# Last stage of an attention, PReLU and soft-mixture kernel: VectorE block transposes, nine output buffers, and unread identity products between the last products

## The chip, the core and the metric

The kernel runs as one program on one core of a Trainium2 chip. The metric is the device time of one execution in microseconds (us), lower is better; three runs of the kernel before are known. A profile of one further execution shows every engine: TensorE (PE, with its weight loads apart as PEld), VectorE (DVE), ScalarE (ACT), GpSimd (POOL) and SyncE (SP), which issues all DMAs.

## What is computed

Three layers in fp32, for 4608 tokens of 512 features:

```python
q_p, k_p = phi(q), phi(k)                # exp features, 8 batches x 8 heads x 576 tokens
x = (q_p @ (k_p.T @ v)) / (q_p @ z)      # linear attention
h = x @ w_in
g = np.maximum(h, 0.0) + alpha * np.minimum(h, 0.0)
x = g @ w_out
logits = x @ phi                         # 32 slots: 8 experts x 4
d = softmax(logits, axis=0)              # over the tokens
slot_input = d.T @ x                     # 32 x 512
h = np.maximum(slot_input[e] @ w1[e], 0.0)
slot_out[e] = h @ w2[e]                  # per expert, 4 slots each, w1 512x1024, w2 1024x512
c = softmax(logits, axis=1)              # over the slots
out = c @ slot_out                       # 4608 x 512
```

## The kernel before

The tokens are taken in 12 blocks of 384. In a slot, one of 16 columns of `w_in` is multiplied with a block (L505), put through the leaky function on ScalarE and VectorE into `gT`, and block-transposed on VectorE into `gb` (L532); the dispatch softmax keeps running sums in `acc` and `lsum`, which each block rescales by `sc` (products `pS`, L602, added at L614). This loop takes nearly the whole time. The text here is on what follows the last block.

- **The reduction.** After the last block's logits (`pl` L540, `pr` L558) VectorE transposes `dT` into `d`, TensorE forms `pS` (96 products of 32x32 tiles), VectorE adds them into `acc` (L614), and TensorE sums the four quarters of `acc` with a folding matrix `tident` (`pg`, L757), each followed by a ScalarE copy to `aT` (L759). `px` (L762) multiplies with `w_out`; `lsum` scales it (L768); `psi` (L769) folds it into the slot inputs `sT`.
- **The experts.** `pe` (L782) multiplies `sT` with `w1`: 64 products of 128 rows by 512 columns into four column strips of the array. ScalarE applies the ReLU (L784), TensorE turns the result (`pth`, L790), and VectorE places each expert's own four slots into a zeroed `hTm` (L793). `pso` (L819) multiplies with `w2`, 64 products of 256 columns for each half `dh` of the output features.
- **The output.** The combine weights (`combine`, on VectorE) are split into high and low halves (`cr`, L803, L805), turned on TensorE (`pc`, L808) and copied to `cT` (L810). For each half, `so` (L823) and `prp` (L825) give `sor`, and 36 products `po` (L836) of one weight load and 256 columns each go out over copies into `os` (L839 and L841, 512 columns each) and one 512 KB DMA for each of nine `os` tiles (L842). `os` has three buffers.

All DMAs stand in one queue, SP's, in the program's order. `fetch` (L686) loads the weights in 144 pieces of 256 KB: 16 of `w_out`, 64 of `w1`, 64 of `w2`. The first 100 go to buffers that the loop has left; the last 44, all of `w2`, wait for buffers of earlier pieces that have been read, in the order that `reuse` gives. The output's DMAs stand behind them.

`spin(count, before)` (L105) issues products of the identity with itself that nobody reads, chained to their neighbours by `together`, so that TensorE is not idle. The order of instructions on each engine is made by the scheduler of the framework from its own model of times.

Of the kernel before, what the change touches and what calls it, by code (L numbers as in the profile page):

```python
# [9 lines left out]
F32 = mybir.dt.float32  # L10
# [16 lines left out]
BT = 384  # L27
# [16 lines left out]
SPIN = [5, 3, 13, 6]  # L44

F64_LEAST = struct.unpack("<f", struct.pack("<I", 0x38100000))[0]
# [15 lines left out]
def attention_prelu_softmoe(ctx: ExitStack, tc, qT, kT, v, wphi, w_in, w_out, alpha, phi, w1, w2, out):  # L62
# [39 lines left out]
    def spin(count, before):  # L102
        turn = bank("spin", ps_d)
# [33 lines left out]
    acc = const.tile([128, 4, 512], F32, name="acc")  # L137
# [409 lines left out]
    gemm_last, spun = [None], [None]  # L547

    def softmax(step, n):
# [39 lines left out]
        def turn():  # L589
            d = st["d"] = sm.tile([128, 512], F32, tag="d", name="d")[:, 0:BT]  # L590
            nc.vector.transpose(out=d, in_=st["dT"])
            for r in range(4):
                sl = slice(32 * r, 32 * r + 32)
                nc.vector.transpose(  # L594
                    out=logits[sl, TB * n:TB * n + TB, :],
                    in_=st["pr"][sl, 0:BT].rearrange("p (t r i) -> p t r i", t=TB, r=4)[:, :, r])

        def gather():
            two = banks("pS")
            pS = st["pS"] = [bank("pS"), bank("pS"), two[:, 0], two[:, 1]]  # L600
            last = together([
                lambda j=j, i=i, h=h: nc.tensor.matmul(  # L602
                    pS[i][32 * (j % 4):32 * (j % 4) + 32, 256 * h:256 * h + 256], st["d"][32 * i:32 * i + 32, 32 * j:32 * j + 32],
                    gb[n, h][32 * i:32 * i + 32, :, 32 * j:32 * j + 32], start=(j < 4), stop=(j >= 4 * TB - 4))
                for h in (1, 0) for j in range(4 * TB) for i in range(4)], spun[0] if n == NB - 1 else None)
            if n == NB - 1:
                spun[0] = spin(SPIN[3], last)

        def add():
            for i in range(4):  # L610
                if st["first"]:
                    nc.vector.tensor_copy(acc[:, i], st["pS"][i])
                else:
                    nc.vector.scalar_tensor_tensor(out=acc[:, i], in0=acc[:, i], scalar=st["sc"], in1=st["pS"][i], op0=ALU.mult, op1=ALU.add)  # L614
# [5 lines left out]
        at_step(step + 2, "pe2", gather)  # L620
        at_step(step + 2, "post", add)
# [37 lines left out]
    at(NC * (NB - 1) - 6, "post", lambda: combine(0, NT - 2 * TB))  # L659
    at(NC * (NB - 1) + 8, "post", lambda: combine(NT - 2 * TB, NT - TB))  # L660
# [5 lines left out]
    pieces += [("w2", dh, e, c) for dh in range(2) for e in range(E) for c in range(EF // 256)]  # L666
    got, groups = {}, []

    def fetch(pool, tag, count=1, bufs=1, whole=None):
# [3 lines left out]
        for i in range(count):  # L673
# [8 lines left out]
            else:  # L682
                _, dh, e, c = key
                t = t.rearrange("p (c d) -> p c d", c=2)
                src = w2[e, 256 * c:256 * c + 256, 256 * dh:256 * dh + 256].rearrange("(c p) d -> p c d", p=128)
# [56 lines left out]
    kept = ["klo", "kraw", "khi", "vte", "vto", "kp1", "ks", "pf0", "pf1", "kp2", "pf2", "pf10", "pf11", "pf12", "pf13", "w8", "w9", "w10", "gb", "gT"]  # L742
# [8 lines left out]
    pg, px, psi = bank("pg"), bank("px"), bank("psi")  # L751
    sT = sm.tile([128, BT], F32, tag="dT", name="sT")[:, 0:KD * NSL].rearrange("p (k s) -> p k s", k=KD)
    aT = sm.tile([128, 512], F32, tag="d", name="aT")
    for i in range(4):
        o = slice(128 * i, 128 * i + 128)
        spun[0] = together([
            lambda c=c: nc.tensor.matmul(pg[:, 128 * i + 32 * c:128 * i + 32 * c + 32], acc[:, i, 128 * c:128 * c + 128], tident[:, 0:32], start=True, stop=True)  # L757
            for c in range(4)], spun[0])
        nc.scalar.copy(aT[:, o], pg[:, o])  # L759
    for i in range(4):  # L760
        spun[0] = together([
            lambda c=c: nc.tensor.matmul(  # L762
                px[32 * c:32 * c + 32, :], aT[:, 128 * i + 32 * c:128 * i + 32 * c + 32], got["wo", 4 * i + c], start=(i == 0), stop=(i == 3))
            for c in range(4)], spun[0])
    acc = acc[:, 0]
    for k in range(KD):
        o = slice(128 * k, 128 * k + 128)
        nc.scalar.activation(acc[:, o], px[:, o], AF.Identity, scale=lsum)  # L768
        nc.tensor.matmul(psi[:, 32 * k:32 * k + 32], acc[:, o], tident[:, 0:32], start=True, stop=True)  # L769
        nc.scalar.copy(sT[:, k, :], psi[:, 32 * k:32 * k + 32])  # L770

    hTm = [attk.tile([128, 4, E, NSL], F32, tag="kp2", name="hTm", bufs=KPB) for f in range(2)]
    for t in hTm:
        nc.gpsimd.memset(t, 0.0)
    hrs = attk.tile([128, 2, 512], F32, tag="kp2", name="hrs", bufs=KPB)
    hr_t = {}
    for eg in range(2):
        for fh in range(2):
# [4 lines left out]
            hr = hr_t[eg, fh] = hrs[:, fh, :]  # L783
            nc.scalar.activation(hr, pe, AF.Relu)  # L784
            if (eg, fh) == (0, 0):
                continue
            for g2, f2 in ([(0, 0), (0, 1)] if (eg, fh) == (0, 1) else [(eg, fh)]):
                pt = bank("pth")
                for c in range(4):
                    nc.tensor.transpose(pt[:, 128 * c:128 * c + 128], hr_t[g2, f2][:, 128 * c:128 * c + 128], ident)  # L790
                for j in range(4):
                    e = 4 * g2 + j
                    nc.vector.tensor_copy(  # L793
                        hTm[f2][:, :, e, 4 * e:4 * e + 4],
                        pt.rearrange("p (c s) -> p c s", c=4)[:, :, 32 * j + 4 * e:32 * j + 4 * e + 4])

    combine(NT - TB, NT)
    cT_t = []
    for i in range(NT // 4):
        cr = pf.tile([128, 4, 4, NSL], F32R, tag=f"pf{PF - 4 + i % 2}", name="cr")  # L800
        lg = logits[:, 4 * i:4 * i + 4, :]
        for r in range(2):
            nc.vector.tensor_copy(cr[:, :, r, :], lg)  # L803
        for r in range(2):
            nc.vector.tensor_tensor(out=cr[:, :, 2 + r, :], in0=lg, in1=cr[:, :, r, :], op=ALU.subtract)  # L805
        pc = bank("pc").rearrange("p (t s) -> p t s", t=4)
        for t in range(4):
            nc.tensor.transpose(pc[:, t, :], cr[:, t].rearrange("p r s -> p (r s)").bitcast(F32), ident)  # L808
        cT = (attk if i < 7 else pf).tile([128, 4, 128], F32R, tag=kept[i], name="cT")
        nc.scalar.copy(cT, pc)  # L810
        cT_t.append(cT)

    so2 = pf.tile([128, 2, 256], F32, tag="pf12", name="so")
    sor2 = pf.tile([128, 2, 256], F32R, tag="pf13", name="sor")
    for dh in range(2):
        pso = (ps_l, ps_d)[dh].tile([128, 512], F32, tag="ld"[dh], name="pso")[:, 0:256]
        for e in range(E):
            for c in range(EF // 128):
                nc.tensor.matmul(  # L819
                    pso[32 * (c % 4):32 * (c % 4) + 32, :], hTm[c // 4][:, c % 4, e, :], got["w2", dh, e, c // 2][:, c % 2, :],  # L820
                    start=(e == 0 and c < 4), stop=(e == E - 1 and c >= 4))
# [6 lines left out]
        for r in (1, 3):  # L828
            sl = slice(32 * r, 32 * r + 32)
            nc.vector.tensor_tensor(out=sor[sl], in0=prp[sl], in1=sor[sl], op=ALU.subtract)  # L830
        for i in range(NT // 4):
            os_ = wring.tile([128, 4, 256], F32, tag=f"w{8 + i % 3}", name="os")
            for t2 in range(2):
                po = (ps_h.tile([128, 512], F32, tag="h", name="po") if (2 * i + t2) % 2 else bank("po"))
                for t in range(2):
                    nc.tensor.matmul(po[:, 256 * t:256 * t + 256], cT_t[i][:, 2 * t2 + t, :], sor, start=True, stop=True)  # L836
                pv = po.rearrange("p (t d) -> p t d", t=2)
                if t2:
                    nc.vector.tensor_copy(os_[:, 2:4], pv)  # L839
                else:  # L840
                    nc.scalar.copy(os_[:, 0:2], pv)  # L841
# [56 lines left out]
```

## Time and profile before

| | |
|---|---|
| three runs | 1056.34, 1056.88, 1061.24 us (median 1056.88) |
| profiled execution | 1057.16 us, its span 1055.4 us |
| busy share of the span | PE 93%, DVE 73%, ACT 45%, POOL 14% |
| mean granted TensorE clock | 0.964 of 2.4 GHz |
| DMA | 110.60 MB |

The span is from the first to the last instruction of the program; times below are counted from its start. A busy PE is not a PE at its peak, as products are pipelined and their ends are modelled; the distance between two starts is the better measure.

### The profile page before, as it was taken

The page shows a single profiled execution, that of the slowest core. Times are in us where ns is not written, and L with a number is a line of the kernel's source. Part 1 is how long each engine was busy: PE and PEld are TensorE (multiplying, and loading weights), DVE is VectorE, ACT ScalarE, POOL GpSimd, SP SyncE. Part 2 cuts the span into 40 slices and gives each one's busy share as a digit, 9 for nine tenths or more (in the row PEclk, how much of TensorE's full clock was granted, in tenths as well). Part 3 has the DMA queues.
Part 4 walks back from the last instruction along what each step waited for, and adds up shares of the span by engine and source line. Part 5 has one row for each costly group of instructions (what it writes and reads, how often), then busy time and mean ns, then how long its engine had stood idle before and what let it go on. Part 6 is the DMA issues. An engine that isn't in the chain of part 4 may idle for free.

```text
span 1055.4 us, 21864 instructions
## 1 busy us (share of the span) xinstructions
PE 984.1 (93%) x9038; PEld 685.2 (65%) x9038; DVE 773.8 (73%) x1552; ACT 469.8 (45%) x908; POOL 149.2 (14%) x88
## 2 busy tenths in 40 slices
PE   3787998998999999999999999999999999998994
PEld 1445776774676776676666776767667767787353
DVE  3999989879767578587878687687888486874133
ACT  3876867776444245144235344343334343200133
POOL 2201214121111212121112111121112221000000
PEclk7898999998999999999999999999999999999995
DMA  5343653653010111010401111110401200769879
GB/s 199 120 141 125 193 188 114 225 178 100 9 31 31 39 31 38 20 51 19 163 10 38 32 39 31 31 38 19 160 19 46 96 8 2 249 226 327 261 235 309
DMA packets 71986, 110.60 MB, mean 105 GB/s; under 512 B 7248, under 2 KB 47312, under 8 KB 71888
## 3 DMA queue, kind: packets, MB, share of 16 engines
q1 hardware_dynamic: 71888, 109.22, 32.0%
q8 instruction: 71, 1.16, 0.4%
q14 instruction: 27, 0.22, 0.1%
HBM read 89.27 MB, written 19.92 MB: 103 GB/s over the span
## 4 chain that ended last, share of the span: by engine, by line
PE 71%; DVE 3%; DMA 2%; ACT 1%; issue 1%; DVEq 0%; ACTq 0%; SPq 0%
PE ph L505 34%; PE num L435 5%; PE pS L602 5%; PE pkv L333 5%; PE pl L540 4%; PE den L442 3%; PE pq L403 3%; PE pk L289 2%; DMA out_dram<-os 2%; PE pso L819 1%; PE pe L782 1%; PE sel L477 1%; PE pt L355 1%; PE pr L558 1%; PE densum L460 1%; PE pkv L339 1%
## 5 line engine op out<-in xcount | busy, mean ns | idle before, releaser
L505 PE MATMUL ph<-xhi,w 128*128 128x384 f32 x1536 | 435.2, 351 | 6.5 <-DVE gT L515 4.4
L505 PEld LDWEIGHTS ph<-xhi,w 128*128 128x128 f32 x1536 | 279.0, 189 | 76.8 <-issue 41.5
L505 PE MATMUL ph<-xlo,w 128*128 128x384 f32 x768 | 255.1, 340 | 0.0
L415 POOL PARTITION_ALL_REDUCE mb<-pj x48 | 140.4, 2928 | 553.0 <-ACT pj L409 450.1
L505 PEld LDWEIGHTS ph<-xlo,w 128*128 128x128 f32 x768 | 143.6, 188 | 12.6 <-issue 6.1
L515 DVE SCALAR_TENSOR_TENSOR gT<-gT,alpha_neg,ph 128x384 f32<-128x384 f32 x104 | 62.9, 605 | 77.3 <-ACT ph L514 76.5
L532 DVE STREAM_TRANSPOSE gb<-gT 128x384 f32<-128x384 f32 x192 | 105.6, 566 | 5.7 <-DMA gT<-gT_d 1.9
L513 ACT ACTIVATE gT<-ph 128x384 f32<-128x384 f32 x104 | 50.8, 489 | 114.8 <-PE ph L505 114.0
L425 ACT ACTIVATE qe<-pj 128x768 f32<-128x768 f32 x92 | 73.9, 839 | 59.5 <-DVE pj L419 56.2
L517 DVE TENSOR_SCALAR gT<-ph,alpha_sb 128x384 f32<-128x384 f32 x88 | 53.8, 613 | 46.2 <-PE ph L505 45.8
L333 PE MATMUL pkv<-kp,vt 128*64 128x256 f32 (+1 forms) x640 | 85.0, 400 | 1.1 <-DVE wpr L250 1.1
L435 PE MATMUL num<-qe,kv 128*64 128x192 f32 (+1 forms) x496 | 70.9, 417 | 0.0
L283 ACT ACTIVATE kp<-kp 128x512 f32<-128x512 f32 (+1 forms) x80 | 46.8, 586 | 51.6 <-DVE kp L282 51.1
L333 PEld LDWEIGHTS pkv<-kp,vt 128*64 128x64 f32 (+1 forms) x640 | 41.3, 140 | 39.4 <-issue 17.1
L280 DVE TENSOR_REDUCE mx<-pk 128x4 f32<-128x512 f32 (+1 forms) x80 | 50.2, 627 | 11.4 <-PE pk L289 9.7
L602 PE MATMUL pS<-gb,d 32*32 32x256 f32 x2304 | 55.0, 385 | 0.3 <-DVE logits L594 0.2
L403 PE MATMUL pq<-qraw,wp 64*128 64x384 f32 x192 | 48.9, 562 | 6.7 <-DMA qraw<-in_qT_dram 4.1
L446 ACT COPY num<-num 128x384 f32<-128x384 f32 x48 | 22.8, 475 | 67.1 <-PE num L435 64.2
L409 ACT COPY pj<-pq 128x768 f32<-128x768 f32 x44 | 35.2, 799 | 36.3 <-PE pq L403 36.3
L419 DVE TENSOR_TENSOR pj<-pj,mb 128x768 f32<-128x768 f32 x48 | 46.6, 971 | 6.0 <-POOL mb L415 6.0
L282 DVE TENSOR_TENSOR kp<-pk,mx 128x512 f32<-128x512 f32 (+1 forms) x80 | 50.2, 627 | 0.8 <-PE pkv L333 0.2
L514 ACT ACTIVATE ph<-ph 128x384 f32<-128x384 f32 x104 | 50.6, 487 | 0.0
(191 smaller groups left out, 1345.6 us busy)
## 6 DMA issues: line engine op xcount, KB each, us to landing
w<-in_w_dram SPq DMA_DIRECT2D x58, 256.0 KB, 5.7
qraw<-in_qT_dram SPq DMA_DIRECT2D x48, 192.0 KB, 2.4
out_dram<-os SPq DMA_DIRECT2D x18, 512.0 KB, 3.7
raw<-in_w_in_dram SPq DMA_DIRECT2D x16, 512.0 KB, 3.6
raw<-in_w_out_dram SPq DMA_DIRECT2D x16, 512.0 KB, 4.2
gT_d<-gT SPq DMA_DIRECT2D x32, 192.0 KB, 2.0
gT<-gT_d SPq DMA_DIRECT2D x8, 768.0 KB, 5.2
pf<-in_w_dram SPq DMA_DIRECT2D x21, 256.0 KB, 6.0
```

Of the source, the lines that this page charges most:

```text
L333: return lambda: nc.tensor.matmul(pkv[64 * j:64 * j + 64, 0:256], vt[:, 64 * j:64 * j + 64], feats(t, j).rearrange("p s f -> p (s f)"), st ...
L403: lambda j=j, sl=slice(64 * j, 64 * j + 64): nc.tensor.matmul(pq[j][:, 0:BT], wp[sl], st["qraw"][sl], start=True, stop=True)
L415: nc.gpsimd.partition_all_reduce(mb, pj, 128, bass_isa.ReduceOp.absmax)
L425: nc.scalar.activation(st["e", s], pj, AF.Exp, scale=(1.0, -1.0)[s])
L435: lambda s=s, j=j: nc.tensor.matmul(num[64 * j:64 * j + 64, o:o + w], kvs[:, s, 64 * j:64 * j + 64], st["e", s][:, j, o:o + w], start=(s = ...
L505: gemm_last[0] = nc.tensor.matmul(h, (w_in_hi, w_in_lo)[a][c][:, 128 * k:128 * k + 128], (xhi, xlo)[b][:, k, :], start=(i == 0), stop=(i = ...
L513: nc.scalar.activation(gT, h, AF.Relu, scale=-1.0)
L514: nc.scalar.activation(h, h, AF.Relu)
L515: nc.vector.scalar_tensor_tensor(out=gT, in0=gT, scalar=alpha_neg[:, c:c + 1], in1=h, op0=ALU.mult, op1=ALU.add)
L517: nc.vector.tensor_scalar(out=gT, in0=h, scalar1=0.0, scalar2=alpha_sb[:, c:c + 1], op0=ALU.min, op1=ALU.mult)
L532: nc.vector.transpose(out=gb[n, c // 8][:, c % 8, :], in_=gT)
L602: lambda j=j, i=i, h=h: nc.tensor.matmul(pS[i][32 * (j % 4):32 * (j % 4) + 32, 256 * h:256 * h + 256], st["d"][32 * i:32 * i + 32, 32 * j: ...
```

## The change

It rebuilds what follows the last block, in these parts:

1. The old `acc` is rescaled on TensorE before the last `pS` (`carry`: products `pa` of `acc` with `tsc`, which is `tident` times `sc`), and `pS` is copied into `acc` on both engines and folded into the same `pa`. `pg` is four transposes, copied in two halves.
2. The ReLU and the masking of foreign slots are one VectorE instruction (`own` holds the mask, ten small reductions); the turns of `pth` and `pc` on TensorE become 32x32 block transposes on VectorE, and `combine` leaves its result block-transposed in `logits`. `pso` takes the rows of `w2` in another order, so each piece is read from DRAM with other strides: a partition's two rows of 1 KB, the next partition 64 KB on.
3. `po` multiplies without the split in halves: `sor` and `logits` are plain fp32, each product has 32 rows, and two stand side by side in different row strips of the array, into two banks. Behind each pair stand three identity products into a bank that nobody reads (`SPIN[8]`). Two copies of 256 columns follow each pair, one on each engine.
4. `os` has nine buffers, `w7` to `w15`; the pieces of `w2` that wait go into other ones, and the buffers of `w_out` come first.
5. More identity products stand in the reduction (`SPIN[3]` to `SPIN[7]`).

```diff
-SPIN = [5, 3, 13, 6]
+SPIN = [5, 3, 8, 3, 8, 5, 5, 5, 3]
...
+        def carry():
+            tsc = sm.tile([128, BT], F32, tag="ls", name="tsc")[:, 0:32]
+            nc.vector.tensor_scalar(out=tsc, in0=tident[:, 0:32], scalar1=st["sc"], scalar2=None, op0=ALU.mult)
+            pa = last["pa"] = ps_h.tile([128, 512], F32, tag="h", name="pa")
+            spun[0] = spin(SPIN[3], together([
+                lambda i=i: nc.tensor.matmul(pa[32 * i:32 * i + 32, :], tsc, acc[i], start=True, stop=False)
+                for i in (3, 2, 1, 0)], spun[0]))
+            gather()
+            for i in range(4):
+                (nc.scalar.copy if i % 2 else nc.vector.tensor_copy)(acc[i], st["pS"][i])
...
-        nc.vector.tensor_tensor(out=lg, in0=lg, in1=wide, op=ALU.mult)
...
+        for t in range(first, last, 16):
+            ts = slice(t, min(t + 16, last))
+            w = sm.tile([128, 512], F32, tag="gT", name="cw", bufs=5).rearrange("p (t s) -> p t s", s=NSL)[:, 0:ts.stop - t]
+            nc.vector.tensor_tensor(
+                out=w, in0=logits[:, ts], in1=cm[:, ts].unsqueeze(2).to_broadcast([128, ts.stop - t, NSL]), op=ALU.mult)
+            nc.vector.transpose(out=logits[:, ts], in_=w)
...
-                src = w2[e, 256 * c:256 * c + 256, 256 * dh:256 * dh + 256].rearrange("(c p) d -> p c d", p=128)
...
+                src = w2[4 * eg:4 * eg + 4].rearrange("e (f b) d -> (e f) b d", b=32)[:, 2 * b:2 * b + 2, 256 * dh:256 * dh + 256]
...
-    kept = ["klo", "kraw", "khi", "vte", "vto", "kp1", "ks", "pf0", "pf1", "kp2", "pf2", "pf10", "pf11", "pf12", "pf13", "w8", "w9", "w10", "gb", "gT"]
+    kept = ["kp2", "pf12", "pf13", "gb", "gT"] + [f"w{c}" for c in range(7, NC)]
...
+    pa = last["pa"]
+    spun[0] = spin(SPIN[5], together([
+        lambda i=i: nc.tensor.matmul(pa[32 * i:32 * i + 32, :], tident[:, 0:32], acc[i], start=False, stop=True)
+        for i in range(4)], spun[0]))
...
+    spun[0] = spin(SPIN[6], together([
+        lambda c=c: nc.tensor.transpose(pg[:, 128 * c:128 * c + 128], acc[c // 2][:, 128 * c:128 * c + 128], ident)
+        for c in range(4)], spun[0]))
+    nc.scalar.copy(aT[:, half[0]], pg[:, half[0]])
+    nc.vector.tensor_copy(aT[:, half[1]], pg[:, half[1]])
+    spun[0] = spin(SPIN[7], together([
+        lambda i=i, c=c: nc.tensor.matmul(
+            px[32 * c:32 * c + 32, :], aT[:, 128 * c + 32 * i:128 * c + 32 * i + 32], got["wo", 4 * i + c], start=(i == 0), stop=(i == 3))
+        for i in range(4) for c in range(4)], spun[0]))
...
-            nc.scalar.activation(hr, pe, AF.Relu)
...
+                out=hr[:, 512 * fh:512 * fh + 512], in0=pe, scalar1=0.0, scalar2=own[:, 4 + eg:5 + eg], op0=ALU.max, op1=ALU.min)
...
+                out=t[b].rearrange("p (b s) -> p b s", s=32),
+                in_=hr.rearrange("p (f b) -> p b f", b=32)[:, 16 * b:16 * b + 16])
...
-            nc.tensor.transpose(pc[:, t, :], cr[:, t].rearrange("p r s -> p (r s)").bitcast(F32), ident)
...
-    sor2 = pf.tile([128, 2, 256], F32R, tag="pf13", name="sor")
+    sor2 = pf.tile([128, 2, 256], F32, tag=f"pf{PF - 1}", name="sor")
...
-            os_ = wring.tile([128, 4, 256], F32, tag=f"w{8 + i % 3}", name="os")
-            for t2 in range(2):
-                po = (ps_h.tile([128, 512], F32, tag="h", name="po") if (2 * i + t2) % 2 else bank("po"))
-                for t in range(2):
-                    nc.tensor.matmul(po[:, 256 * t:256 * t + 256], cT_t[i][:, 2 * t2 + t, :], sor, start=True, stop=True)
...
+            os_ = wring.tile([128, 4, 256], F32, tag=f"w{7 + i}", name="os")
+            for h in range(2):
+                k = (2 * i + h) % 3
+                two = banks("po") if k == 2 else None
+                po = [two[:, j] if k == 2 else bank("po") if k else ps_h.tile([128, 512], F32, tag="h", name="po") for j in range(2)]
+                last[dh] = spin(SPIN[8], together([
+                    lambda j=j, r=2 * h + j, sl=slice(64 * h + 32 * j, 64 * h + 32 * j + 32): nc.tensor.matmul(
+                        po[j][:, 0:256], logits[sl, 4 * i:4 * i + 4, :].rearrange("p t s -> p (t s)"), sor[sl], start=True, stop=True)
+                    for j in range(2)], last.get(dh)), idle)
+                for j in range(2):
+                    (nc.vector.tensor_copy if j else nc.scalar.copy)(os_[:, 2 * h + j], po[j][:, 0:256])
```

Names of tiles in the rows that follow are the program's own; a number behind one is a buffer's.

On TensorE, the kernel before ends its second half of `pso` and then issues the two output halves in one piece each:

```order
L819 MATMUL pso<-w_10248,hTm 32x256 x4
L819 MATMUL pso<-w_10251,hTm 32x256 x4
L819 MATMUL pso<-w_10254,hTm 32x256 x4
L836 MATMUL po<-sor,cT 128x256 x36
L825 MATMUL prp<-so,tident 128x256
L836 MATMUL po<-sor,cT 128x256 x36
```

At the same place the changed kernel has:

```order
L828 MATMUL pso<-num,acc_112 32x256 x6
L828 MATMUL pso<-rhl,acc_113 32x256 x2
L828 MATMUL pso<-densel,acc_113 32x256 x2
L828 MATMUL pso<-w_10248,acc_113 32x256 x3
L846 MATMUL po<-sor,logits 128x256 x2
L106 MATMUL idle<-ident 128x128 x3
L846 MATMUL po<-sor,logits 128x256 x2
L106 MATMUL idle<-ident 128x128 x3
```

The last two rows come 18 times in all, and only then follow the last 25 products of the second half's `pso`, its `prp`, and 18 such pairs again. So the first output half now stands ahead of the end of `pso` on TensorE.

On TensorE after the last block's logits, the kernel before has:

```order
L558 MATMUL pr<-ls,tident 128x384
L105 MATMUL spin<-ident 128x128 x13
L602 MATMUL pS<-gb,d 32x256 x96
L105 MATMUL spin<-ident 128x128 x6
L757 MATMUL pg<-tident,acc 128x32 x16
```

and the changed kernel:

```order
L559 MATMUL pr<-ls,tident 128x384
L106 MATMUL spin<-ident 128x128 x8
L623 MATMUL pa<-acc_114,tsc 32x512
L623 MATMUL pa<-acc_113,tsc 32x512
L623 MATMUL pa<-acc_112,tsc 32x512
L623 MATMUL pa<-acc_111,tsc 32x512
L106 MATMUL spin<-ident 128x128 x3
L604 MATMUL pS<-gb,d 32x256 x96
L106 MATMUL spin<-ident 128x128 x8
```

`pS` now stands behind four products that read `tsc`, and behind three identity products.

On VectorE at that place the changed kernel has the rows below; before, `mrun`, `d`, `logits` and `lsum` followed `sc` with nothing between them.

```order
L579 TENSOR_TENSOR sc<-mrun,nm 128x1
L800 TENSOR_REDUCE own<-ident 128x1 x3
L580 TENSOR_TENSOR mrun<-mbl,mrun 128x1
L800 TENSOR_REDUCE own<-ident 128x1
L802 TENSOR_REDUCE own<-own 128x1
L592 STREAM_TRANSPOSE d<-dT 128x384
L596 STREAM_TRANSPOSE logits<-pr 32x128 x2
L588 SCALAR_TENSOR_TENSOR lsum<-lsum,sc,rs 128x1
L596 STREAM_TRANSPOSE logits<-pr 32x128
L620 TENSOR_SCALAR tsc<-tident,sc 128x32
```

Five reductions moved ahead of `d`, and `tsc` stands last.

## Rows read from the trace of the kernel before

**Rows 1.** By stage: us, busy us of PE, PEld, DVE, ACT, POOL, PEclk, DMA share, GB/s

```profile
966.00:981.30 15.30, 12.29 (x76) 7.95 (x76) 2.67 (x4) 1.06 (x4) 0.00 (x0) 0.78 0.76 242
...
1000.10:1022.80 22.70, 22.70 (x304) 12.36 (x303) 7.46 (x39) 6.25 (x11) 0.00 (x0) 1.00 0.80 253
1022.80:1055.40 32.60, 16.99 (x74) 13.32 (x74) 13.63 (x21) 10.73 (x19) 0.00 (x0) 0.66 0.87 290
```

**Rows 2.** Chain of waits after the loop: start us, us, what (x instructions)

```profile
961.97 3.99 PE pS L602 x173
...
968.08 1.83 issue
...
976.30 5.02 PE px L762 x32
...
984.88 0.34 PE psi L769 x2
...
987.41 3.57 PE pe L782 x32
...
1000.72 1.86 PE pso L819 x32
...
1017.44 0.59 PE pc L808 x4
...
1019.88 0.63 PE prp L825 x2
...
1022.79 1.63 PE po L836 x10
```

**Rows 3.** Waits after 950 us: who waited for whom: us, times, longest

```profile
ACT os L841 <- DMA out_dram<-os: 12.5, 11, 2.4
```

**Rows 4.** By stage again, a stretch of 4 us within the output

```profile
1044.00:1048.00 4.00, 2.97 (x10) 2.38 (x11) 1.80 (x3) 1.46 (x3) 0.00 (x0) 0.50 1.02 343
```

**Rows 5.** Timeline of TensorE at 956 us: start us, us, engine line op

```profile
956.60 0.94 PE L105 MATMUL spin<-ident 128*128 128x128 f32 x6
957.38 0.91 PE L558 MATMUL pr<-ls,tident 128*128 128x384 f32 x2
958.13 3.06 PE L105 MATMUL spin<-ident 128*128 128x128 f32 x26
961.12 0.40 PE L602 MATMUL pS<-gb,d 32*32 32x256 f32 x1
```

**Rows 6.** Timeline of TensorE at 399 us, a pair in row strips

```profile
399.18 0.34 PE L478 MATMUL sel<-rhl,densel 128*128 128x384 f32 x1
399.45 0.92 PE L403 MATMUL pq<-qraw,wp 64*128 64x384 f32 x4
400.30 0.44 PE L505 MATMUL ph<-xhi,w 128*128 128x384 f32 x1
```

**Rows 7.** Timeline of VectorE after 959 us

```profile
959.17 0.16 DVE L578 TENSOR_TENSOR sc<-mrun,nm 128x1 f32<-128x1 f32 x1
...
959.94 0.58 DVE L591 STREAM_TRANSPOSE d<-dT 128x384 f32<-128x384 f32 x1 [0.41 <-ACT dT L581]
...
962.81 0.25 DVE L654 TENSOR_REDUCE cm<-logits 128x3 f32<-128x96 f32 x1 [0.35 <-ACT logits L653]
```

**Rows 8.** Timeline of SP, the DMA issues

```profile
980.37 2.93 SPq L686 DMA_DIRECT2D vg<-in_w_dram  x6
...
993.03 19.86 SPq L686 DMA_DIRECT2D w<-in_w_dram  x26
```

**Rows 9.** DMA issues after 890 us: KB each, median us to landing

```profile
w<-in_w_dram SPq DMA_DIRECT2D x58, 256.0 KB, 5.7
out_dram<-os SPq DMA_DIRECT2D x18, 512.0 KB, 3.7
```

**Rows 10.** Timeline, copies of 256 columns

```profile
1012.26 0.42 DVE L823 COPY so<-pso 128x256 f32<-128x256 f32 x1 [0.65 <-PE pso L819]
...
1020.54 0.37 ACT L827 CAST sor<-prp 128x256 fp32r<-128x256 f32 x1 [1.89 <-PE prp L825]
```

More of the change, by code (lines that the diff above doesn't have):

```diff
@@ L100, in together, with spin @@
         return before
-    def spin(count, before):
-        turn = bank("spin", ps_d)
+    def spin(count, before, turn=None):
+        turn = turn or bank("spin", ps_d)
         return together([
@@ L136, in attention_prelu_softmoe @@
     wpr = sm.tile([128, NC, NSL], F32, tag="wpr", name="wpr")
-    acc = const.tile([128, 4, 512], F32, name="acc")
+    acc = [const.tile([128, 512], F32, name=f"acc{i}") for i in range(4)]
     lsum = const.tile([128, 1], F32, name="lsum")
@@ L546, in attention_prelu_softmoe @@
     first = [True]
-    gemm_last, spun = [None], [None]
+    gemm_last, spun, last = [None], [None], {}
     def softmax(step, n):
@@ L591, in turn @@
             nc.vector.transpose(out=d, in_=st["dT"])
-            for r in range(4):
-                sl = slice(32 * r, 32 * r + 32)
+            for i in range(TB):
+                g, j = divmod(TB * n + i, 4)
+                sl = slice(32 * j, 32 * j + 32)
                 nc.vector.transpose(
-                    out=logits[sl, TB * n:TB * n + TB, :],
-                    in_=st["pr"][sl, 0:BT].rearrange("p (t r i) -> p t r i", t=TB, r=4)[:, :, r])
+                    out=logits[sl, 4 * g:4 * g + 4, :],
+                    in_=st["pr"][sl, 128 * i:128 * i + 128].rearrange("p (t i) -> p t i", i=32))
         def gather():
@@ L600, in gather @@
             pS = st["pS"] = [bank("pS"), bank("pS"), two[:, 0], two[:, 1]]
-            last = together([
+            end = together([
                 lambda j=j, i=i, h=h: nc.tensor.matmul(
@@ L606, in gather @@
             if n == NB - 1:
-                spun[0] = spin(SPIN[3], last)
+                spun[0] = spin(SPIN[4], end)
         def add():
@@ L665, in attention_prelu_softmoe @@
     pieces += [("w1", eg, fh, k, j) for eg in range(2) for fh in range(2) for k in range(KD) for j in range(4)]
-    pieces += [("w2", dh, e, c) for dh in range(2) for e in range(E) for c in range(EF // 256)]
+    pieces += [("w2", dh, eg, i) for dh in range(2) for eg in range(2) for i in range(16)]
     got, groups = {}, []
@@ L760, in attention_prelu_softmoe @@
[L760 to L765, printed above, removed]
-    for k in range(KD):
[L767 to L776, printed above, removed]
-    for eg in range(2):
+    pa = last["pa"]
+    spun[0] = spin(SPIN[5], together([
+        lambda i=i: nc.tensor.matmul(pa[32 * i:32 * i + 32, :], tident[:, 0:32], acc[i], start=False, stop=True)
+        for i in range(4)], spun[0]))
+    half = [slice(0, 256), slice(256, 512)]
@@ new lines, in attention_prelu_softmoe @@
+    nc.scalar.copy(acc[0][:, half[0]], pa[:, half[0]])
+    nc.vector.tensor_copy(acc[1][:, half[1]], pa[:, half[1]])
+    pg, px, psi = bank("pg"), bank("px"), bank("psi")
+    spun[0] = spin(SPIN[6], together([
[7 more added lines that the diff above has]
+        for i in range(4) for c in range(4)], spun[0]))
@@ new lines, in attention_prelu_softmoe @@
+    nc.scalar.activation(acc[2][:, half[0]], px[:, half[0]], AF.Identity, scale=lsum)
+    nc.vector.tensor_scalar(out=acc[3][:, half[1]], in0=px[:, half[1]], scalar1=lsum, scalar2=None, op0=ALU.mult)
+    for k in range(KD):
+        nc.tensor.matmul(psi[:, 32 * k:32 * k + 32], acc[2 + k // 2][:, 128 * k:128 * k + 128], tident[:, 0:32], start=True, stop=True)
+    nc.scalar.copy(sT, psi[:, 0:KD * NSL].rearrange("p (k s) -> p k s", k=KD))
+    own = sm.tile([128, 8], F32, tag="sc", name="own", bufs=2)
@@ new lines, in attention_prelu_softmoe @@
+    for eg in range(2):
+        for j in range(4):
+            nc.vector.tensor_reduce(
+                out=own[:, j:j + 1], in_=ident[:, 36 * j + 16 * eg:36 * j + 16 * eg + 4], axis=AX.X, op=ALU.add)
+        nc.vector.tensor_reduce(out=own[:, 4 + eg:5 + eg], in_=own[:, 0:4], axis=AX.X, op=ALU.add)
+    nc.vector.tensor_scalar(out=own[:, 4:6], in0=own[:, 4:6], scalar1=F32_MOST, scalar2=None, op0=ALU.mult)
+    hT = []
+    for eg in range(2):
+        hr = attk.tile([128, EF], F32, tag="kp2", name="hr", bufs=KPB)
@@ L815, in attention_prelu_softmoe @@
+        hT.append(t)
+    combine(NT - 4, NT)
+    so2 = pf.tile([128, 2, 256], F32, tag=f"pf{PF - 2}", name="so")
+    sor2 = pf.tile([128, 2, 256], F32, tag=f"pf{PF - 1}", name="sor")
     for dh in range(2):
         pso = (ps_l, ps_d)[dh].tile([128, 512], F32, tag="ld"[dh], name="pso")[:, 0:256]
-        for e in range(E):
-            for c in range(EF // 128):
+        for eg in range(2):
+            for b in range(32):
                 nc.tensor.matmul(
-                    pso[32 * (c % 4):32 * (c % 4) + 32, :], hTm[c // 4][:, c % 4, e, :], got["w2", dh, e, c // 2][:, c % 2, :],
-                    start=(e == 0 and c < 4), stop=(e == E - 1 and c >= 4))
+                    pso[32 * (b % 4):32 * (b % 4) + 32, :], hT[eg][b // 16][:, 32 * (b % 16):32 * (b % 16) + 32],
+                    got["w2", dh, eg, b // 2][:, b % 2, :], start=(eg == 0 and b < 4), stop=(eg == 1 and b >= 28))
```

66 lines of the change are left out of this document (17 added, 49 removed).

## The prediction

> **What bounds the kernel now.** Only what follows the last block changes much, so I read the stages of the tail first, then its chain of waits, then the rows from which the new instructions can be priced. Between 1000.1 and 1022.8 us TensorE is busy without a gap, at the full clock, while the DMAs have room [rows 1]: there TensorE's own list of instructions is the bound. From 1022.8 us to the end it is the other way round: TensorE is busy for half of the time, and the copies wait for the output's DMAs, ScalarE's alone 12.5 us in eleven waits, because `os` has three buffers [rows 1, 3]. The DMAs then move 343 GB/s [rows 4], which is 1.53 us for one `os` of 512 KB, 27.5 us for eighteen. The reader is to see that the present output stage of 32.6 us is 27.5 us of DMA and 5 us of starting, turning from one half to the other, and landing. A change that adds TensorE work there costs nothing until an `os` takes TensorE more than 1.53 us.
>
> **The price of a pass.** A fp32 product runs as two passes. 26 identity passes of 128 columns take 2.99 us up to the next product's start [rows 5], and the last of them includes a change to another tiling of the array. A change costs 0.10: from `sel` to `pq` it is 0.27 us [rows 6], where a single-rate pass of 384 columns takes 0.17 by the same rate. So a pass of 128 columns is (2.99 - 0.10)/26 = 0.111 us, one of 256 is 0.222.
>
> **The new output pairs.** The nearest row is the pair `pq`, which stands side by side in two row strips: its two passes of 384 columns take 0.85 us to the start of the next product [rows 6], against 2 x 0.333 of streaming, so 0.18 goes to its second weight load and to the way back. The first identity product after a change of tiling costs 0.11 more: six passes take 0.78 instead of 0.67 [rows 5]. One `po` pair with three identity products behind it is then 0.10 + 0.44 + 0.18 + 0.11 + 6 x 0.111 = **1.50 us**. Bounds: 1.11, if the changes of tiling were free, to 1.60, if row strips of 32 rows switch a little worse than those of 64. I take 1.50, as the row is the same kind of pair. An `os` needs two pairs, 3.0 us, about twice what its DMA needs. The copies (0.42 and 0.37 us for 256 columns, one on each engine [rows 10]) hide behind a pair, and nine buffers take the waits of rows 3 away, but these were the DMA's own time, not an extra one. So TensorE becomes the bound of the output: 18 x 1.50 = 27.0 us for each half.
>
> **The reduction.** I follow it on the times of before. Eight identity products end at 958.13 + 1.78 = 959.9. `pa` needs `tsc`, last on VectorE: `sc` is at 959.17, then come five small reductions ahead of `d` (bounds 0.1 to 0.25 each, a reduction of 96 columns taking 0.25 [rows 7]; I take 0.18, as they have four columns), so `d` starts at 960.5 instead of 959.94; `d` and three block transposes, `lsum` and `tsc` put `tsc` at about 962.4. TensorE waits 2.5 us there. Then `pa` is 8 passes of 512 columns in column strips, 0.9 us (32 such passes of `pe` take 3.57 [rows 2]), three identity products 0.8, and `pS` starts at 964.1, two microseconds later than before [rows 2], and ends at 968.1. What follows is better than before: 1.9 (eight identity products, over the two copies of 512 columns on each engine) + 0.9 `pa` + 1.2 + 0.6 for four transposes (as `pc` [rows 2]) + 1.2 + 3.6 for `px` (32 passes like `pe`; before, the clock was at half for a part, 0.78 on average, after a wait of 1.83 us, and `px` took 5.0 [rows 1, 2]). `px` ends at 977.5, before at 981.3. Identity products 1.2, `psi` 4 x 0.34 [rows 2] with its copy, and `pe` starts at 980.2. Its 128 passes take 14.3 us: 994.5.
>
> **The experts.** `pth` and `pc` leave TensorE: nine `pc` of 0.59 us [rows 2] and four `pth` like them, 7.7 us. The block transposes that replace them are VectorE's (0.77 us for 512 columns, from 0.58 for 384 [rows 7]) and hide behind `pe` and the first 32 products of `pso`, which take 3.7 us; without that cover the last two would cost 1.5. `pso` is 128 passes a half, 4 x 1.86 = 7.4 us [rows 2]: first half done at 1002.0. By the order, 39 products of the second half (4.5 us) and `prp` (0.63 [rows 2], and two changes) come next: the first `po` starts at 1007.3, against 1022.8 before, **15.5 us earlier**. It must not wait for weights: the last piece that those 39 read is the 32nd of the 44 late ones. The first of them wait for `px` alone, which starts at 974, where before SP stood until 980.4 [rows 8]; at 0.76 us a piece (19.86/26 [rows 8]) and 5.7 to landing [rows 9] the 32nd is there at 974 + 24.3 + 5.7 = 1004. Two microseconds of cover.
>
> **The end.** First half 27.0: 1034.3. The remaining 25 products of `pso`, 2.9: 1037.2. `so`, `prp`, `sor` with handovers, 1.6: 1038.8. Seventeen periods and a last pair, 26.2: 1065.0. A copy 0.4 and the last DMA 3.7 [rows 9]: 1069.1, so 13.7 us after the end of before. In the loop, `combine` adds two block transposes of 512 and 384 columns, 1.35 us of VectorE between leaky steps: from nothing, hidden behind a buffered `ph`, to 1.35; I take 0.7. Sum: 1057.16 + 13.7 + 0.7 = 1071.6 for the profiled execution, which lay 0.3 above the median: **1071 us**.
>
> **The rivals.**
> - *The changes of tiling cost nothing here* (1.11 us a pair). For it: identity and pair need different weights anyway, and loads can overlap. Against: 0.10 and 0.18 in rows 6. 36 x 0.39 = 14 us less: 1057, no change. The Trainium skill's page "TensorEngine Tiling (Array Packing)", section "Key Properties", says that changing the mode drains the engine; by that rule this rival falls, and rows 6 agree with it, 0.10 us for one change.
> - *The output stays with the DMA queue*, the one on the other side. If the identity products did not hold the pairs up, so that a pair came in less than 0.77 us, the eighteen `os` would follow each other at 1.53 from 1008 on: 1008 + 1.5 + 27.5 + 3.7 = 1041 in the span's time, and 1043 us. For it: that is what bounds the stage now, and the nine buffers would let the first half leave while `pso` goes on. Against: 0.67 of identity passes and 0.44 of the pair's own stand in one list, 1.11 together.
> - *The late pieces of `w2` come slowly*, as neighbouring partitions now read 64 KB apart. A quarter slower (1.0 us a piece) brings the 32nd at 1013 and costs 6 us beyond the cover; half the rate, 1.52, brings it at 1029 to 1034 and costs 23: 1094. For it: nothing in this trace reads with such strides. Against: runs stay 1 KB long. The Trainium skill's page "DMA: Bandwidth & Descriptors", section "Latency and other measured facts", has copies at full rate (207 GB/s) with rows 512 KiB apart and at half (103) with 4 MiB; 64 KB is not in it, and experts stand 2 MB apart. By it an estimate lies anywhere from no loss to the 1094. No run here shows it yet.
> - *The clock falls in the output*, as it did before (0.50 [rows 4]). Pairs would take 3.0 us: 1125. Against: in the stage from 1000.1 us, where TensorE's list also runs without a gap, the clock stayed at 1.00 [rows 1]; at 0.50 TensorE mostly waited for copies.
>
> **How the numbers follow.** The forecast has 0.70, free changes 0.11, the DMA-bound end 0.05, slow pieces 0.10, a low clock 0.04. The forecast's own range is 1064 to 1079: 1.40 to 1.60 for a pair is -4 to +4, the reductions and the loop +-1.5, a fall of the clock in the 2.5 us wait up to +4. The range 1057 to 1083 takes in the free changes and pieces up to a quarter slower. A difference of 0.5% (5.3 us) is about what runs of this kernel can tell. Faster 0.05 (DMA-bound), within it 0.11 (free changes), slower 0.84.
>
> **What would show it.** Right: starts of `po` pairs 1.50 us apart with the clock at 1.00; PE without gaps from 980 to 1065; the first `po` near 1007 and the second half near 1039; no wait of an `os` copy for a DMA; DMA share near a half in the output; `pS` starting two microseconds later and `px` ending four earlier. Wrong: pairs 1.1 us apart or less; copies that wait for `out`; a PE gap ahead of `pso` ended by a DMA; a clock of 0.50 after 1007.

## The result, and the profile after

| | |
|---|---|
| changed kernel, 4 runs | 1070.06, 1072.04, 1073.61, 1075.21 us, median 1072.82 |
| kernel before, 4 runs beside it | median 1057.89 us |
| ratio | 1.0135, 95% interval [1.0107, 1.0162] |
| profiled execution | 1072.04 us, its span 1070.3 us, mean granted clock 0.975 |

The change makes the kernel 1.35% slower, 15 us; 1071 was forecast. Comparisons here and below leave disturbed runs out.

The changed kernel by stage (start and end; length, busy us of PE, PEld, DVE, ACT, POOL, clock, DMA share, GB/s):

```profile
966.00:981.30 15.30, 14.00 (x220) 9.37 (x190) 2.62 (x5) 2.48 (x6) 0.00 (x0) 1.00 1.03 327
...
994.50:1007.30 12.80, 12.80 (x220) 9.90 (x212) 3.73 (x6) 0.37 (x1) 0.00 (x0) 1.00 1.04 338
1007.30:1034.30 27.00, 27.00 (x184) 18.78 (x180) 7.55 (x18) 6.71 (x18) 0.00 (x0) 1.00 0.65 219
1034.30:1039.00 4.70, 3.89 (x53) 1.97 (x52) 0.51 (x2) 0.17 (x1) 0.00 (x0) 1.00 0.35 115
...
1044.00:1048.00 4.00, 4.00 (x29) 2.76 (x28) 0.96 (x3) 1.12 (x3) 0.00 (x0) 1.00 0.51 170
```

Before, TensorE waited for half of the output, and the DMAs moved 290 GB/s over the whole stage and 343 in the stretch of rows 4 [rows 1, 4]. Now it is the reverse: in the first output half TensorE is busy for 27.0 of 27.0 us, at the full clock, while the DMAs move 219 GB/s, the last weights included. The bound has moved from the DMA queue to TensorE's list.

Its chain of waits (start us, us, what):

```profile
956.15 0.85 PE pl L541 x8
...
962.13 0.25 DVE tsc L620
962.43 1.06 PE pa L623 x8
...
964.36 3.94 PE pS L604 x173
...
970.06 1.12 issue
...
975.42 3.57 PE px L788 x32
...
981.53 14.01 PE pe L811 x128
995.54 8.99 PE pso L828 x166
...
1007.45 0.63 PE po L846 x4
1008.08 0.86 PE idle L106 x6
1008.95 0.63 PE po L846 x4
...
1034.38 3.15 PE pso L828 x50
...
1039.26 0.70 PE po L846 x4
...
1065.84 0.42 DVE os L850
```

From 981 to 1066 us the chain hardly leaves TensorE. A pair of `po` takes 0.63 us and its three identity products 0.86 us; the distance between two of a half's eighteen pairs is 1.50 us. The first pair comes 15.3 us earlier than `po` did before [rows 2], and each half then takes 27 us.

Its waits after 954 us (who waited for whom: us, times, longest):

```profile
ACT os L850 <- PE po L846: 41.5, 36, 2.5
...
PE pa L623 <- DVE tsc L620: 2.0, 1, 2.0
```

No copy waits for a DMA of the output, where ScalarE alone waited 12.5 us before [rows 3]; all 36 of ScalarE's copies wait for TensorE. One copy on VectorE waits 1.4 us for a DMA of the weights.

### The profile page after: what moved, and what is told of

It reads as the page before. It is cut to its first block, busy times and chain, and to the rows that moved or that the text cites. A ratio compares the mean times of both kernels' runs of the same rounds, so it can differ in the third digit from the quotient of the medians.

```text
span 1070.3 us, 22297 instructions
## 1 busy us (share of the span) xinstructions
PE 1010.4 (94%) x9292; PEld 708.9 (66%) x9292; DVE 773.9 (72%) x1528; ACT 464.9 (43%) x907; POOL 147.2 (14%) x86
## 4 chain that ended last, share of the span: by engine, by line
PE 74%; DVE 3%; issue 0%; ACT 0%; DVEq 0%; ACTq 0%
PE ph L506 34%; PE num L436 5%; PE pS L604 5%; PE pkv L334 5%; PE pl L541 3%; PE den L443 3%; PE idle L106 3%; PE pq L404 3%; PE po L846 2%; PE pk L290 2%; PE pso L828 1%; PE pe L811 1%; PE sel L478 1%; PE pt L356 1%; PE pr L559 1%; PE spin L106 1%
## 5 line engine op out<-in xcount | busy, mean ns | idle before, releaser
L506 PEld LDWEIGHTS ph<-xlo,w 128*128 128x128 f32 x768 | 143.7, 188 | 12.6 <-issue 6.1
```

The source lines that it names most:

```text
L506: gemm_last[0] = nc.tensor.matmul(h, (w_in_hi, w_in_lo)[a][c][:, 128 * k:128 * k + 128], (xhi, xlo)[b][:, k, :], start=(i == 0), stop=(i = ...
```

## The experiments

The main theory: in the output, identity products, changes of tiling and the pairs' own passes add up in one list, 1.50 us a pair, and this list has become the bound in place of the DMA queue. The rivals: the identity products only fill time in which something else holds the pairs; or they buy the clock, and the clock decides. Each ratio is against runs of the kernel before on the same chip, with its 95% interval.

**1. No identity products behind the pairs (no_identity).**

```diff
-SPIN = [5, 3, 8, 3, 8, 5, 5, 5, 3]
+SPIN = [5, 3, 8, 3, 8, 5, 5, 5, 0]
```

> The changed kernel without the identity products behind the output pairs (SPIN[8] = 0). My theory: the changed kernel's output is bound by TensorE's own list, 1.50 us a pair, of which 0.67 us are the identity products and 0.39 us the two changes of tiling that they force; without them a pair takes about 0.45 us, an os 0.9 us, less than the 1.53 us of its DMA, and the DMA queue becomes the bound: the last weights land near 1014, 18 times 1.53 us and a landing of 3 us follow, so about 1045 us, 27 us less than the changed kernel and 12 us less than before, with copies or DMA waits where TensorE was busy. Rival 1, that the identity products only fill time in which something else (copies, PSUM, the queue) holds the pairs: no change, 1072 us. Rival 2, that they buy the clock and that the clock decides: TensorE falls to a granted clock of 0.5, a pair and the rest of pso take twice as long, and pairs of 0.9 to 1.2 us plus 25 slow products of pso (5.8 instead of 2.9 us) give at least 1050 us.

Measured: 1046.16 us, ratio 0.9889 [0.9863, 0.9916], 27 us less than the changed kernel, and faster than before. The theory gave 1045, and the first rival falls. The second is only half tested here: the products do not buy the clock, as it stays at 1.00 up to 1032 us without them, but what a low clock costs is left to experiment 5. Its queue of DMA issues (start us, us) and two of its stages:

```profile
1010.21 29.16 SPq L851 DMA_DIRECT2D out_dram<-os  x18
```

```profile
1018.00:1021.00 3.00, 2.77 (x20) 1.18 (x20) 1.06 (x3) 0.99 (x4) 0.00 (x0) 1.00 0.16 55
1021.00:1039.00 18.00, 12.30 (x102) 7.91 (x102) 10.07 (x28) 8.54 (x28) 0.00 (x0) 0.91 1.00 332
```

From 1021 us the DMAs are full and TensorE waits again: the queue is the bound. But in the three microseconds before, the DMAs are nearly idle while TensorE works. Its timeline of TensorE shows why (a product of `po` is x2, a pair x4):

```profile
1016.10 0.69 PE L846 MATMUL po<-sor,logits 32*128 32x256 f32 x2
1016.73 0.63 PE L828 MATMUL pso<-w,acc 128*32 128x256 f32 x4
1017.28 0.69 PE L846 MATMUL po<-sor,logits 32*128 32x256 f32 x2
1017.91 0.62 PE L828 MATMUL pso<-w,acc 128*32 128x256 f32 x2
1018.46 0.69 PE L846 MATMUL po<-sor,logits 32*128 32x256 f32 x2
```

Without identity products the scheduler puts pieces of the second half's `pso` between the pairs of the first half, and here between the two products of a pair, and each piece costs at least 0.55 us. A product of `po` comes every 1.18 us, so an `os`, which needs four, takes 4.7 us, against 1.53 of its DMA. Experiment 7 takes this up.

**2. One identity product behind each pair (one_identity).** The edit is that of the first experiment, with 1 as the last number.

> The changed kernel with one identity product instead of three behind each output pair (SPIN[8] = 1). My theory, that passes and changes of tiling add up in one list: the period of a pair falls by 2 times 0.223 us from 1.496 to 1.05 us; an os takes 2.1 us, still above the 1.53 us of its DMA, so TensorE stays the bound, and each half gets 18 times 0.446 = 8.0 us shorter: 1073 - 16 = 1057 us, within 2 us. If the changes of tiling were free and something else made up the 0.39 us, the period would be 0.67 us and the queue the bound: 1045 us. If pairs are held by something else: 1072 us.

Measured: 1060.3 us, ratio 1.0035 [1.0001, 1.0068]; its profiled execution took 1059.97 us. That is three more than expected, a little outside the two microseconds allowed. Its timeline of TensorE:

```profile
1006.71 0.70 PE L846 MATMUL po<-sor,logits 32*128 32x256 f32 x4
1007.34 0.49 PE L106 MATMUL idle<-ident 128*128 128x128 f32 x2
1007.76 0.70 PE L846 MATMUL po<-sor,logits 32*128 32x256 f32 x4
1008.39 0.49 PE L106 MATMUL idle<-ident 128*128 128x128 f32 x2
1008.81 0.70 PE L846 MATMUL po<-sor,logits 32*128 32x256 f32 x4
```

The period is 1.05 us, as expected: (1.496 - 1.05)/2 = 0.223 us for each identity product, and 0.82 for the pair with its changes of tiling, 0.38 above the pair's own 0.44 us of passes. The three microseconds that are missing are again pieces of `pso` between the output's products, from 1009.9 us on: the eight pieces take 5.7 us, where the changed kernel's one piece took 3.15.

**3. The same products with half of the changes (regrouped).** Two pairs stand together, and then six identity products.

```diff
-                last[dh] = spin(SPIN[8], together([
+                last[dh] = spin(2 * SPIN[8] * h, together([
```

> The changed kernel with the two output pairs of an os directly behind each other and then all six identity products, where there were three behind each pair. The number of products is the same; the changes of tiling are halved. From the changed kernel and from one identity product (periods 1.496 and 1.047 us) an identity product costs 0.224 us and what is left of a pair 0.823 us; two pairs in four row strips run side by side without identity products (four products in 0.54 us). My theory, that the 0.38 us above the pair's own 0.44 us belong to the changes of tiling: an os takes about 0.64 us to its first identity product and 1.54 us for six, 2.2 us instead of 2.99, 18 times 0.8 us less: 1058 us. The rival, that the overhead belongs to each pair and its weights and not to the change: 2.99 us an os and no change, 1072 us.

Measured: 1059.44 us, ratio 1.0015 [0.9999, 1.0031], 13 us less than the changed kernel with the same number of products. Its chain of waits:

```profile
1005.47 0.64 PE po L846 x8
1006.12 1.54 PE idle L106 x12
1007.65 0.64 PE po L846 x8
```

An `os` now takes 2.18 us instead of 2.99, as expected. The gain is not all changes of tiling: four products take 0.64 us, hardly more than two, so the second pair streams beside the first in the other two row strips. By the prices above, 0.44 us of the gain are the second pair's own passes, and 0.38 is one round of changes: 0.19 at the pair, and 0.19 at the identity products, of which six take 1.54 us instead of 2 x 0.86. Identity products behind each pair thus cost more than their own passes: they keep two pairs from running side by side.

**4. Three `os` buffers instead of nine (three_buffers), and 5. the same without identity products (no_identity_three_buffers).**

```diff
-            os_ = wring.tile([128, 4, 256], F32, tag=f"w{7 + i}", name="os")
+            os_ = wring.tile([128, 4, 256], F32, tag=f"w{7 + i % 3}", name="os")
```

> The changed kernel with three os buffers instead of nine, identity products as they are. My theory: an os comes every 3.0 us and its DMA lands 3.0 us after the issue, so three buffers come round after 9 us and no copy waits; no change, 1072 to 1073 us. If the nine buffers give the changed kernel something, copies wait for the DMAs again, above all in the first four os, whose DMAs stand behind the last weights until 1010 to 1014 us: 2 to 4 us more.

Measured: 1070.65 us, ratio 1.0127 [1.0103, 1.0151]: no difference to nine buffers (1.0135), and no copy waits for a DMA of the output. With TensorE as the bound, the buffers give nothing.

> No identity products behind the output pairs, and three os buffers. My theory: now the DMA is the bound, and a buffer comes free only with its DMA, so copies wait as in the kernel before, where the stage of 18 os took 32.6 us against 27.5 us of pure transfer; about 4 us more than without the identity products and with nine buffers, so about 1049 us, and copies that wait for out. If buffers are worth nothing even here: 1045 us. If the identity products were no bound: 1072 us or more.

Measured: 1047.27 us, ratio 0.9906 [0.9882, 0.9929]. Four microseconds were expected against nine buffers, one was found, within the intervals. Copies do wait, and the clock falls:

```profile
ACT os L850 <- DMA out_dram<-os: 8.1, 8, 1.7
```

```profile
1026.00:1032.00 6.00, 5.92 (x41) 4.26 (x43) 3.12 (x8) 2.69 (x8) 0.00 (x0) 0.50 0.80 270
1032.00:1039.00 7.00, 6.23 (x38) 3.50 (x31) 3.41 (x9) 2.97 (x9) 0.00 (x0) 0.50 1.01 340
```

Here the granted clock is 0.50 from 1026 us on, and the time is still 26 us below that of the changed kernel at 1.00, and 1.1 us above that of experiment 1, where the clock was 1.00 up to 1032 us. So in this stage the clock is worth about a microsecond at most, and experiment 1 keeps it without identity products.

**6. The reduction without its new identity products (plain_reduction).**

```diff
-SPIN = [5, 3, 8, 3, 8, 5, 5, 5, 3]
+SPIN = [5, 3, 8, 0, 0, 0, 0, 0, 3]
```

> The changed kernel without the identity products that it adds in the reduction (SPIN[3] to SPIN[7] = 0; those of SPIN[2] and those of the output stay). My theory: they mostly fill waits for copies. Those behind pS even hold pa up, as the copies into acc end at 969.6 and pa starts at 971.6; without them pa starts up to 2 us earlier, but TensorE waits, the clock can fall as it did in the kernel before (0.78, px 5.0 instead of 3.6 us), and the two cancel: 1070 to 1074 us. The rival, that the clock falls to 0.5 and stays there into pe: px and pe take up to 3 and 7 us longer, at least 1077 us. If the identity products cost and the clock does not care: 1069 us.

Measured: 1071.07 us, ratio 1.0120 [1.0082, 1.0158]: no difference that the times can show, as expected, but not for the reason given. Its stage of the reduction and its chain there:

```profile
966.00:981.30 15.30, 12.63 (x198) 5.57 (x190) 2.62 (x5) 2.65 (x6) 0.00 (x0) 1.00 1.09 347
```

```profile
957.28 0.85 PE pl L541 x8
...
964.61 3.96 PE pS L604 x171
...
969.30 2.27 PE pa L776 x8
...
973.38 4.11 PE px L788 x31
...
979.60 5.43 PE pe L811 x48
```

The clock did not fall at all (1.00, where before it was 0.78 [rows 1]), although TensorE waited. `pa` starts 0.7 us after `pS` instead of 3.3 behind identity products and a wait. Some of that is lost again, as its passes are spread over the copies of `acc` and `px` takes 4.1 us instead of 3.6. What is left shows when the trace is read from the last block's `pl` on: `pe` starts 22.3 us later here and 25.4 in the changed kernel, and the span ends 111.2 and 114.2 us later. In the other eight executions with these identity products `pe` starts 24.2 to 25.7 us after `pl`, and in that of experiment 10, which has none, 22.3. So they cost about two microseconds at `pe`, as the last reading of the expectation has it. The times hide this, because the loop ahead is not the same in every execution: in the changed kernel and its ten variants that `pl` starts between 955.0 and 958.3 us.

**7. The pairs first (pairs_first).** No identity products in the output, and the last 24 products of the second half's `pso` are held behind the first half's last pair.

```diff
+                if dh and eg and b >= 8:
+                    tc.add_manual_dep(mm.ins, last[0].name, nosync, reason="behind the first half")
```

> No identity products behind the output pairs, and the last 24 products of the second half's pso held behind the last output pair of the first half, so that they do not stand between the pairs. Without the hold the pairs of the first half came in 11 us, 0.55 us of pso between them, and the DMA queue was empty for about 2.5 us at 1019. My theory, that the queue is the bound from the first os on: this gap goes, and nine os keep the queue busy until about 1027, while the rest of pso, so, prp and sor need until about 1021: 1044 us, 2 us less. The rival, that the end is set by something else (the landing of the last weights, the order of the halves): 1046 us, the gap only moves behind the first half.

Measured: 1041.67 us, ratio 0.9848 [0.9824, 0.9872]; 1044 was expected. Its stages, and its queue of DMA issues:

```profile
1007.00:1013.00 6.00, 6.00 (x77) 3.36 (x71) 2.57 (x7) 2.60 (x9) 0.00 (x0) 1.00 1.10 351
1013.00:1020.00 7.00, 6.18 (x72) 3.99 (x76) 4.13 (x12) 3.33 (x11) 0.00 (x0) 1.00 1.08 381
1020.00:1026.00 6.00, 4.88 (x57) 3.04 (x50) 2.27 (x6) 2.09 (x7) 0.00 (x0) 1.00 1.06 362
1026.00:1032.00 6.00, 4.82 (x43) 3.13 (x41) 4.03 (x12) 3.54 (x12) 0.00 (x0) 1.00 1.03 351
1032.00:1039.00 7.00, 0.41 (x4) 0.01 (x2) 0.75 (x2) 0.37 (x1) 0.00 (x0) 0.73 1.04 341
```

```profile
1010.64 24.48 SPq L853 DMA_DIRECT2D out_dram<-os  x18
```

The gap is gone: the DMAs stay full from the late weights to the end, and TensorE has hardly anything left to do after 1032 us. That it came out two microseconds better than expected goes in part with the rate: the 9.33 MB that the DMAs moved from 1013 to 1039 us would take 27.2 us at the 343 GB/s assumed [rows 4], 1.2 more. The rest is no more than executions differ by ahead of the last block.

**8. Near rows of `w2` (near_rows).** On the kernel of the first experiment:

```diff
-                src = w2[4 * eg:4 * eg + 4].rearrange("e (f b) d -> (e f) b d", b=32)[:, 2 * b:2 * b + 2, 256 * dh:256 * dh + 256]
+                e, c = 4 * eg + b // 4, b % 4
+                src = w2[e, 256 * c:256 * c + 256, 256 * dh:256 * dh + 256].rearrange("(c p) d -> p c d", p=128)
```

> No identity products behind the output pairs, and each piece of w2 read as the kernel before read it (a partition's two rows 128 rows apart, neighbouring partitions 2 KB apart, instead of 64 KB); the rows of w2 then stand in the wrong order for the products, so the output is not the reference's. The DMA queue bounds the end in this variant, so slower pieces show in the time. My theory: rows 64 KB apart cost nothing (the late pieces moved at 334 to 350 GB/s in every stage): no change, 1046 us. The rival, slow pieces: 64 of them a quarter slower than 0.76 us would be 12 us, and 1034 us here; a tenth would be 5 us, 1041 us.

Measured: 1046.02 us, ratio 0.9887 [0.9860, 0.9914], against 0.9889 with rows 64 KB apart. From 995 to 1007 us this kernel's DMAs move 350 GB/s, those of the first experiment's 349:

```profile
995.00:1007.00 12.00, 12.00 (x207) 9.14 (x201) 3.24 (x7) 0.96 (x4) 0.00 (x0) 1.00 1.10 350
```

The new strides cost nothing that can be measured.

**9. The pairs first, with three buffers (pairs_first_three_buffers).** The edit of experiment 4 on the kernel of experiment 7.

> As pairs_first (no identity products behind the output pairs, the last pso products behind the first half's pairs), with three os buffers instead of nine. With the pso products between the pairs three buffers cost only about 1 us, where I had expected 4. My theory: there the pairs came so slowly in the first half that a buffer was free anyway. With the pairs first they are held only by copies and buffers, so now a copy waits for the DMA three os earlier, the pairs of the first half hold the pso products behind them up until the DMAs are through, and the queue runs empty between the halves: 1046 to 1049 us against 1041.7 with nine buffers. The rival, that the number of buffers does not matter once the queue bounds the stage: 1042 us.

Measured: 1048.35 us, ratio 0.9909 [0.9892, 0.9926], 6.7 us more than with nine buffers, as expected. The wait and the gap are both there:

```profile
ACT os L852 <- DMA out_dram<-os: 12.5, 10, 4.9
```

```profile
1026.00:1032.00 6.00, 4.87 (x50) 3.01 (x42) 2.27 (x6) 2.20 (x7) 0.00 (x0) 0.96 0.12 42
```

Of the three kernels tried with three buffers and with nine, this is the only one in which the nine have a worth that shows: the pairs outrun the queue, and `pso` stands behind them.

**10. No new identity products at all (no_identity_at_all).** `SPIN = [5, 3, 8, 0, 0, 0, 0, 0, 0]` on the kernel of experiment 7.

> As pairs_first, and also without the identity products of the reduction (SPIN[3] to SPIN[7] = 0). In the changed kernel these made no measurable difference, whose TensorE list is the bound from pe to the end. My theory: with the queue as the bound from the last weights to the end (348 to 380 GB/s without a gap in pairs_first) the reduction is covered by the weights' DMAs and nothing changes: 1041 to 1042 us. The rival, that a lower clock in the reduction and in pe delays the first os beyond the last weights at 1011: 1044 us or more.

Measured: 1039.59 us, ratio 0.9822 [0.9806, 0.9838], the fastest of all. It is 2 us below experiment 7, where no change was expected; the two intervals still overlap. The traces point the way of experiment 6: `pe` starts 22.3 us after `pl` instead of 25.7 (of which 1.4 is a wait for an issue that experiment 7's execution has), and the span ends 81.9 us after it instead of 83.5. That the clock has no say is shown once more, against 1.00 in the same stages of experiment 7:

```profile
1020.00:1026.00 6.00, 5.59 (x42) 4.46 (x44) 3.16 (x8) 3.02 (x9) 0.00 (x0) 0.67 1.07 370
1026.00:1032.00 6.00, 5.68 (x33) 3.14 (x30) 3.26 (x9) 3.06 (x9) 0.00 (x0) 0.50 1.06 360
```

## Why the prediction was right

- **The price of a pair, 1.50 us**, was measured as 1.496. Its parts held too: 0.223 for an identity product (two passes of 0.111) and 0.38 for the changes of tiling with their weight loads (0.39 forecast), which `regrouped` and `one_identity` show as separate from the number of passes. One cause was wrong: I gave part of 0.18 us to the pair's second weight load, but a single product between pieces of `pso` takes 0.63 us as well (experiment 1), and four take 0.64 (experiment 3), so that load does not show. The rival of free changes (1.11 us a pair) falls; how much of the 0.38 is the change itself and how much the weight load behind it stays open. The Trainium skill's page "TensorEngine Tiling (Array Packing)", section "Key Properties", says that changing the mode drains the engine; the trace agrees as far as it goes, with 0.38 us for the two changes of a pair.
- **The bound moves from the queue to TensorE**: shown by the first experiment. The rival of a DMA-bound end was priced at 1043 us and comes out at 1046 when the identity products go. So the loss against before is their doing: 1072.8 - 1046.2 = 27 us, against the 12 us that the rest of the change wins; which of its parts win them no run takes apart.
- **The reduction and the experts.** `pa` waits 2.0 us for `tsc` (2.5 forecast), and the clock does not fall in this wait (1.00); `px` ends at 979.0 instead of 977.5 (2.3 us earlier than before, not four), `pe` at 995.5 instead of 994.5, and the first pair starts at 1007.4, as forecast. Two errors cancel: 1.1 us of waiting for the issue of an identity product (experiment 7's execution has 1.4 us there, experiment 8's 0.6, the other six with these products 0.3 at most), and `pso`, whose 206 passes take 0.055 us each instead of 0.058. The five reductions of `own`, for which I charged 0.6 us to the path, cost nothing:

```profile
959.58 0.28 DVE L800 TENSOR_REDUCE own<-ident 128x1 f32<-128x4 f32 x3
...
960.27 0.58 DVE L592 STREAM_TRANSPOSE d<-dT 128x384 f32<-128x384 f32 x1
```

 `d` starts 0.33 us later than before [rows 7], and so does everything in this execution since the last block (0.33 us, 0.7 forecast for the loop): the reductions lie in the wait for `dT`.
- **What I took for a reason and wasn't.** I took the identity products of the reduction to hold the clock up and so to shorten `px`. Experiment 6 has neither these nor a lower clock, and the products cost about two microseconds there. Before, TensorE was busy for 1.6 of the 4 us from 968 us on, and the clock was 0.51 in the next four; in experiment 6 its waits behind `pS` are of 0.7 us and less. Whether that is what keeps the clock stays open, as no run takes the rest of the new reduction apart.
- **The rivals.** Slow pieces of `w2` cost nothing (experiment 8). A low clock in the output did not come, and where experiments brought it, it cost about a microsecond at most while the queue was the bound. What the clock would cost with three identity products behind each pair was not tried.
- **The end**: second half at 1039.3 (1038.8 forecast), last copy done at 1066.3, and the last DMA lands with the span's end, 1070.3. The sum was right by its parts: apart from the two errors above and the reductions no term is off by more than half a microsecond. Luck has its share all the same: the two errors cancel, and the loop, for which I took 0.7 us, ends anywhere within 3.3 us from one execution to another (experiment 6). The range of 1064 to 1079 is also not what its parts give, 1065.5 to 1080.5; the measured 1072.8 lies in both.

## What to carry to other kernels

Unread products that are to keep TensorE's clock up are free only where TensorE waits anyway and they end before the wait does. In the reduction they outlast it and cost two microseconds (experiment 6), and in the output the time hardly changed where the clock fell without them (experiments 5 and 10). Count what they add to its list (passes, changes of tiling, and the neighbours that they keep apart) against the period of the engine or queue that bounds the stage. A stage that the DMA queue bounds is won by keeping that queue full, so by what starts its first transfer and by gaps between its parts; TensorE's clock and its order matter there only as far as they open such a gap. More buffers are worth what the producer can run ahead: nothing behind a slow producer, 6.7 us here once the pairs came first.

## What was not expected of the hardware

- Two pairs in four row strips take 0.64 us, one pair 0.63, a single product 0.63: products in different row strips stream side by side, when nothing of another tiling stands between them.
- The DMAs move 381 GB/s in the output's first microseconds (378 from 1016 to 1020 us, with the last weights landed) and 341 at its end (experiment 7), full in both; why stays open.
- In the reduction the clock stayed at 1.00 without any identity product behind `pS` (experiment 6), with TensorE busy for 12.6 of 15.3 us; before, it was busy for 12.3 of them and the clock was 0.78 [rows 1].
